# Reworking the first block's start: x0 by halves, a half-width V group, transposes inside groups, held x loads

## The chip, the cores and the metric

One core of one Trainium2 chip. The metric is the time of one execution in microseconds of device time, measured by repeated runs; the kernel before took 696.94 us (median of three runs, 696.61 to 697.02). The profile's span of an execution is 1.7 to 1.9 us shorter than its time in nearly all runs.

## The reference, cut to what matters

The program is a layer norm, a sliding-window attention with 32 heads, a residual, a second layer norm and a dense SiLU block, over x of 2048 rows by 1024 columns in bfloat16:

```python
qkv = layernorm(x) @ wqkv            # wqkv is 1024 x 3072: Q, K, V
o   = windowed_softmax(q k^T) v      # window 256
h   = x + o @ wo
out = h + silu(layernorm(h) @ w1) @ w2
```

Only the first 512 rows matter below: four tiles of 128 rows (tile 0 to 3) are loaded, normalized, transposed, and multiplied by the V columns of wqkv. Everything later waits for that.

## The kernel before

The loads at the start. All but one are issued by SyncE, in this order:

```python
nc.scalar.activation(out=dummy[:], in_=eps[:], func=ACT.Sqrt)   # loads the table early
load_x(0, 0)                       # 256 KB
load_wqkv(2 * D)                   # V columns 0-511, 1 MB
load_x(0, 1, nc.scalar)
load_x(0, 2)
load_wqkv(2 * D + 512)             # V columns 512-1023, 1 MB
load_x(0, 3)
load_wqkv(0)                       # first Q columns, 1 MB
...
for i in range(11):                # warm-up matmuls on zeros
    nc.tensor.matmul(o_ps[i % 2]..., lhsT=warm[:, 0, 0:P], rhs=warm[:, 0, :], start=True, stop=True)
```

The small tiles and the big buffers come from pools:

```python
small = ctx.enter_context(tc.tile_pool(name="small", bufs=2))
big = ctx.enter_context(tc.tile_pool(name="big", bufs=1))
...
r_w = big.tile([P, 28672], BF16, name="r_w")     # weights; then r_t, r_o (x), r_a, r_e, r_n
```

The first block. `ln_first` does statistics in two halves on VectorE, the square root on ScalarE, and a normalization in four pieces, so that TensorE can transpose piece by piece; `turn_first` makes eight transposes and four copies on ScalarE; `v_group` is eight matmuls of 512 columns and a copy:

```python
ln_first(x_ring[0], st, rs, 0, None, (x_ring[1], half))   # x1's first half fills the wait for the root
turn_first(x_ring[0], lnT_b[0], 0)
ln_first(x_ring[1], st, rs, 1, half)
v_group(0, 0, 0, act, turn_1)          # turn_1: tile 1's eight transposes before the last matmul
ln_first(x_ring[2], st, rs, 2)
v_group(0, 1, 0, act)
ln_first(x_ring[3], st, rs, 3)
ln_transpose(x_ring[3], lnT_b[0], 3)   # a DMA transpose, issued by SyncE
for c0 in (D, 512, D + 512):
    load_wqkv(c0)
v_group(0, 0, 1, act)
turn_first(x_ring[2], lnT_b[0], 2)
v_group(0, 1, 1, act)
v_group(0, 2, 0, act); v_group(0, 2, 1, act)
... v_group(0, 3, 0, act); v_group(0, 3, 1, act)
for j in range(4):
    load_x(1, j)                       # next block's x, slots 4 to 7
```

The softmax here doesn't subtract the row's maximum and nothing guards it: scores larger than these inputs give would overflow.

## Time and profile before

| what | us |
|---|---|
| time, median | 696.94 |
| span of the profiled run | 695.5 |
| x0 landed | 4.31 |
| first V matmul | 7.98 |
| end of the V phase | 23.26 |

Two rows of the issue table for the end of the first block are added here; the last column is the time from issue to landing.

```profile
r_w<-r_o SPq DMA_TRANSPOSE x1, 2.8
r_w<-in_A_wqkv_dram SPq DMA_DIRECT2D x1, 1024.0 KB, 8.8
```

The first is tile 3's DMA transpose (issued at 16.42), the second the first Q weights (issued at 5.50, so landed at 14.3). In every profile of this study but c3's, whose output was wrong, the span is the end of the V phase plus 672.1 to 672.3 us: what follows the V phase never differs. So a span tells, for any run, when its V phase ended.

### The profile page before, as it was taken

The page shows a single profiled execution, that of the slowest core. Times are in us where ns is not written, and L with a number is a line of the kernel's source. Part 1 is how long each engine was busy: PE and PEld are TensorE (multiplying, and loading weights), DVE is VectorE, ACT ScalarE, POOL GpSimd, SP SyncE. Part 2 cuts the span into 40 slices and gives each one's busy share as a digit, 9 for nine tenths or more (in the row PEclk, how much of TensorE's full clock was granted, in tenths as well). Part 3 has the DMA queues.
Part 4 walks back from the last instruction along what each step waited for, and adds up shares of the span by engine and source line. Part 5 has one row for each costly group of instructions (what it writes and reads, how often), then busy time and mean ns, then how long its engine had stood idle before and what let it go on. Part 6 is the DMA issues. An engine that isn't in the chain of part 4 may idle for free.

```text
span 695.5 us, 12334 instructions
## 1 busy us (share of the span) xinstructions
PE 690.1 (99%) x5091; PEld 331.6 (48%) x5091; DVE 289.5 (42%) x616; ACT 257.9 (37%) x328; POOL 174.5 (25%) x391
## 2 busy tenths in 40 slices
PE   8999999999999999999999999999999999999998
PEld 3444444555555555544444444444444444444445
DVE  6267646644443448544316134433133251244111
ACT  4326657777777777621310023300033100233000
POOL 1007667777777777500000000000000000000000
PEclk9999999999999999999999999999999999999999
DMA  7732131026231778880123410024200023100110
GB/s 241 257 53 77 35 93 51 17 60 193 70 124 23 205 251 272 199 311 31 31 76 99 107 38 1 1 83 77 83 1 1 11 95 91 45 1 1 30 39 24
DMA packets 76457, 60.84 MB, mean 87 GB/s; under 512 B 50288, under 2 KB 60528, under 8 KB 76400
## 3 DMA queue, kind: packets, MB, share of 16 engines
q1 hardware_dynamic: 76256, 59.78, 29.9%
q8 instruction: 40, 0.66, 0.4%
q10 hardware_dynamic: 144, 0.26, 0.1%
q14 instruction: 17, 0.14, 0.1%
HBM read 39.85 MB, written 8.39 MB: 69 GB/s over the span
## 4 chain that ended last, share of the span: by engine, by line
PE 99%; DMA 1%; DVE 0%; issue 0%
PE hacc L563 19%; PE hacc L600 17%; PE acc L248 16%; PE acc L600 10%; PE acc L563 9%; PE acc L238 8%; PE acc L267 7%; PE o_ps L339 4%; PE sc L285 3%; PE hacc L267 1%; PE o_ps L354 1%; PE sc L313 1%; DMA r_o<-in_A_x_dram 1%; PE tp L216 0%; DVE ln_st L169 0%; DVE r_o L197 0%
## 5 line engine op out<-in xcount | busy, mean ns | idle before, releaser
L330 POOL TENSOR_SCALAR_AFFINE_SELECT r_e<-r_e 128x256 bf16<-128x256 bf16 (+1 forms) x384 | 171.6, 477 | 116.5 <-ACT r_e L322 65.1
L293 ACT ACTIVATE r_e<-sc 128x1024 bf16<-128x1024 f32 x144 | 139.5, 1021 | 45.1 <-PE sc L285 31.0
L600 PEld LDWEIGHTS <-r_a 128*128 128x128 bf16 x952 | 90.9, 98 | 103.0
L563 PEld LDWEIGHTS <-r_w 128*128 128x128 bf16 x896 | 87.4, 98 | 104.8
L600 PE MATMUL hacc<-r_a 128*128 128x512 bf16 (+2 forms) x616 | 122.5, 360 | 0.0
L563 PE MATMUL hacc<-r_e,r_w 128*128 128x512 bf16 x456 | 100.9, 379 | 0.0
L572 ACT ACTIVATE r_n<-hacc 128x512 f32<-128x512 f32 x30 | 17.9, 597 | 178.9 <-PE hacc L563 178.9
L600 PE MATMUL acc<-r_a 128*128 128x512 bf16 x336 | 74.0, 379 | 0.0
L248 PEld LDWEIGHTS <-r_w 128*128 128x128 bf16 x512 | 46.5, 97 | 57.1 <-issue 7.0
L250 DVE CAST r_a<-acc 128x512 bf16<-128x512 f32 x56 | 38.7, 691 | 72.9 <-PE acc L248 56.3
L248 PE MATMUL acc<-r_t,r_w 128*128 128x512 bf16 x256 | 60.0, 379 | 0.0
L248 PE MATMUL acc<-r_w 128*128 128x512 bf16 x256 | 58.2, 380 | 0.0
L267 PE MATMUL acc<-r_o,r_a 128*128 128x512 bf16 x208 | 49.4, 380 | 0.0
L563 PE MATMUL acc<-r_e,r_w 128*128 128x512 bf16 x216 | 49.1, 379 | 0.0
L339 PEld LDWEIGHTS <-r_e 128*128 128x128 bf16 x1152 | 39.5, 96 | 17.0
L322 ACT ACTIVATE r_e<-sc 128x1024 bf16<-128x1024 f32 x36 | 34.9, 1021 | 21.2 <-PE sc L313 20.1
L339 PE MATMUL o_ps<-r_a,r_e 128*128 128x33 bf16 x1152 | 40.2, 178 | 0.0
L615 DVE SCALAR_TENSOR_TENSOR r_t<-hacc,r_t 128x512 bf16<-128x512 f32 (+2 forms) x22 | 14.0, 635 | 56.7 <-PE hacc L600 56.7
L267 PEld LDWEIGHTS <-r_a 128*128 128x128 bf16 x256 | 23.1, 98 | 29.6 <-issue 5.1
L615 DVE SCALAR_TENSOR_TENSOR r_t<-acc,r_t 128x512 bf16<-128x512 f32 x12 | 8.3, 692 | 64.2 <-PE acc L600 64.2
L573 DVE SCALAR_TENSOR_TENSOR r_a<-r_n,hacc 128x512 bf16<-128x512 f32 x30 | 20.6, 688 | 33.0 <-ACT r_n L572 33.0
L563 PE MATMUL hacc<-r_a,r_w 128*128 128x512 bf16 x144 | 32.9, 379 | 0.0
(71 smaller groups left out, 476.5 us busy)
## 6 DMA issues: line engine op xcount, KB each, us to landing
r_w<-in_B_w_dram SPq DMA_DIRECT2D x8, 896.0 KB, 5.1
r_a<-in_B_w_dram SPq DMA_DIRECT2D x7, 1024.0 KB, 7.9
r_w<-in_A_wqkv_dram SPq DMA_DIRECT2D x6, 1024.0 KB, 8.7
h_dram<-r_t SPq DMA_DIRECT2D x16, 256.0 KB, 3.0
r_t<-h_dram SPq DMA_DIRECT2D x16, 256.0 KB, 2.8
out_dram<-r_t SPq DMA_DIRECT2D x31, 128.0 KB, 1.7
r_o<-in_A_x_dram SPq DMA_DIRECT2D x15, 256.0 KB, 4.0
r_e<-h_dram SPq DMA_DIRECT2D x3, 1024.0 KB, 5.7
```

The lines of the kernel that those rows point to most:

```text
L238: nc.tensor.matmul(acc, lhsT=lnT_b[b % 2][:, kt, j * P:(j + 1) * P], rhs=wv[:, kt, c * 512:(c + 1) * 512], start=(kt == 0), stop=(kt == KT ...
L248: nc.tensor.matmul(acc, lhsT=wqk[:, kt, col0:col0 + P], rhs=lnT_b[b % 2][:, kt, :], start=(kt == 0), stop=(kt == KT - 1))
L250: copy(out=(qT, kT)[which][b][:, g, :], in_=acc)
L267: nc.tensor.matmul(acc, lhsT=qT[b][:, g, j * P:(j + 1) * P], rhs=wo[:, g, c * 512:(c + 1) * 512], start=(g == 0), stop=(g == G - 1))
L285: nc.tensor.matmul(sc[hh // 2][:, hh % 2, ch * P:(ch + nq) * P], lhsT=kT[t // 4][r0:r0 + DH, g, (t % 4) * P:(t % 4 + 1) * P], rhs=qT[b][r0 ...
L293: nc.scalar.activation(out=e, in_=sc[pair], func=ACT.Exp, scale=scale)
L322: nc.scalar.activation(out=e, in_=sc[pair], func=ACT.Exp, scale=scale)
L330: nc.gpsimd.affine_select(out=ap, in_=ap, pattern=[[0, 2], [0, n], [sgn, P]], compare_op=ALU.is_ge if upper else ALU.is_gt, fill=0.0, base ...
L339: nc.tensor.matmul(o_ps[pair][:, qt * 2 + hh, 0:VW], lhsT=e_of(i, kind, pair)[:, hh, ch * P:(ch + 1) * P], rhs=v[:, b * 4 + kt, g * 4 + pa ...
L563: nc.tensor.matmul(acc, lhsT=w1[:, kt, ft * P:(ft + 1) * P], rhs=ln2T[b][:, kt, :], start=(kt == 0), stop=(kt == KT - 1))
L600: nc.tensor.matmul(acc[:, 0:c1 - c0], lhsT=gT[:, ft, j * P:(j + 1) * P], rhs=w2[ft // 4][:, ft % 4, c0:c1], start=(ft == 0), stop=(ft == F ...
L615: nc.vector.scalar_tensor_tensor(out=t_out[j % 2][:, c0:c1], in0=acc[:, 0:c1 - c0], scalar=0.5, in1=t_in[j % 2][:, c0:c1], op0=ALU.mult, o ...
```

## The change

The intent: start TensorE earlier, by loading x0 in two halves on two queues; keep it busy while VectorE normalizes tile 1, by a V group of 256 columns right after the first; hide transposes inside groups; and keep the next block's x loads out of the way of tile 3's DMA transpose. The diff, cut to its core:

```diff
+    X_SLOT = (0, 0, 4, 0)                     # block 1's x now overwrites block 0's
-    load_x(0, 0)
-    load_wqkv(2 * D)
-    load_x(0, 1, nc.scalar)
-    load_x(0, 2)
-    load_wqkv(2 * D + 512)
+    for queue, c0 in ((nc.sync, 0), (nc.scalar, 512)):
+        queue.dma_start(out=x_ring[0][:, c0:c0 + 512], in_=x2d[0:P, c0:c0 + 512])
+    load_x(0, 1)
+    for queue, k0 in ((nc.scalar, 0), (nc.sync, 4)):
+        queue.dma_start(out=wv[:, k0:k0 + 4, 0:512], in_=wqkv_v[:, k0:k0 + 4, 2 * D:2 * D + 512])
+    for c0, k0, k1 in ((512, 0, 4), (512, 4, 8), (768, 0, 8)):
+        nc.sync.dma_start(out=wv[:, k0:k1, c0:c0 + 256], in_=wqkv_v[:, k0:k1, 2 * D + c0:2 * D + c0 + 256])
+        if c0 == 512 and k0 == 4:
+            load_x(0, 2)
...
-    for i in range(11):
+    for i in range(10):
...
+    quarters = small.tile([P, 4, 6], F32, name="ln_st1", tag="ln_st1")     # tile 1's statistics by quarters
...
+    v_group(0, 0, 0, act)
+    v_cols(0, 0, 512, 768, act, turn_at(1, (3, 5, 7)))
+    turn_first(x_ring[1], lnT_b[0], 1, 3)
+    ln_whole(x_ring[2], st, rs, 2, None, (x_ring[3], half))    # normalized in one piece
     v_group(0, 1, 0, act)
+    ln_whole(x_ring[3], st, rs, 3, half)
     ln_transpose(x_ring[3], lnT_b[0], 3)
+    v_cols(0, 0, 768, 1024, act)
+    v_group(0, 1, 1, act, turn_at(2, (2, 3, 4, 5)))
+    load_x(1, 3)                              # waits for tile 3's transpose; the rest stands behind it
+    load_wqkv(D)
+    for j in range(3):
+        load_x(1, j)
+    for c0 in (512, D + 512):
+        load_wqkv(c0)
```

More of the change, by code (lines that the diff above doesn't have):

```diff
@@ L137, in load_x @@
     def load_x(b, j, queue=nc.sync):
-        queue.dma_start(out=x_ring[(b % 2) * 4 + j], in_=x2d[(b * 4 + j) * P:(b * 4 + j + 1) * P, :])
+        queue.dma_start(out=x_ring[X_SLOT[b] + j], in_=x2d[(b * 4 + j) * P:(b * 4 + j + 1) * P, :])
     def load_wqkv(c0):
@@ L201, in ln_transpose, with ln_first, ln_quarter, ln_whole @@
         nc.sync.dma_start_transpose(out=dst[:, :, j * P:(j + 1) * P], in_=xt)
-    def ln_first(xt, st, rs, j, half_done=None, ahead=None):
+    def ln_first(xt, st, rs, j, stats, ahead=None):
+        nc.vector.bn_aggr(out=st[:, j, :], in_=stats[:])
+        nc.scalar.activation(out=rs[:, j:j + 1], in_=st[:, j, 1:2], func=ACT.Sqrt, bias=eps[:], scale=1.0)
+        if ahead is not None:
+            ahead()
+        nc.vector.reciprocal(out=rs[:, j:j + 1], in_=rs[:, j:j + 1])
+        for h in range(4):
+            ln_norm(xt[:, h * 256:(h + 1) * 256], st, rs, j)
+    def ln_quarter(xt, stats, c):
+        nc.vector.bn_stats(out=stats[:, c, :], in_=xt[:, c * 256:(c + 1) * 256])
+    def ln_whole(xt, st, rs, j, half_done=None, ahead=None):
         ln_stats(xt, st, j, half_done)
@@ L206, in ln_first, with turn_first @@
         if ahead is not None:
-            ln_half(ahead[0], ahead[1], 0)
+            ln_half(*ahead, 0)
         nc.vector.reciprocal(out=rs[:, j:j + 1], in_=rs[:, j:j + 1])
-        for h in range(4):
-            ln_norm(xt[:, h * 256:(h + 1) * 256], st, rs, j)
-    def turn_first(xt, dst, j):
-        for h in range(4):
-            for i in range(2):
-                kt = h * 2 + i
-                nc.tensor.transpose(out=tp_ps[h][:, i * P:(i + 1) * P], in_=xt[:, kt * P:(kt + 1) * P], identity=ident[:])
-            nc.scalar.copy(out=dst[:, h * 2:(h + 1) * 2, j * P:(j + 1) * P],
-                           in_=tp_ps[h][:, 0:256].rearrange("p (k q) -> p k q", q=P))
+        ln_norm(xt, st, rs, j)
+    def turn_first(xt, dst, j, h):
+        for i in range(2):
+            kt = h * 2 + i
+            nc.tensor.transpose(out=tp_ps[h][:, i * P:(i + 1) * P], in_=xt[:, kt * P:(kt + 1) * P], identity=ident[:])
+        nc.scalar.copy(out=dst[:, h * 2:(h + 1) * 2, j * P:(j + 1) * P],
+                       in_=tp_ps[h][:, 0:256].rearrange("p (k q) -> p k q", q=P))
     def ln_tiles(tag):
@@ L231, in next_acc, with v_cols @@
         return acc_banks[acc_n[0] % len(acc_banks)]
-    def v_group(b, j, c, copy, between=None):
-        acc = next_acc()
+    def v_cols(b, j, c0, c1, copy, between=None):
+        acc = next_acc()[:, 0:c1 - c0]
         for kt in range(KT):
@@ L237, in v_group @@
                 between(kt)
-            nc.tensor.matmul(acc, lhsT=lnT_b[b % 2][:, kt, j * P:(j + 1) * P], rhs=wv[:, kt, c * 512:(c + 1) * 512],
+            nc.tensor.matmul(acc, lhsT=lnT_b[b % 2][:, kt, j * P:(j + 1) * P], rhs=wv[:, kt, c0:c1],
                              start=(kt == 0), stop=(kt == KT - 1))
-        copy(out=v[:, b * 4 + j, c * 16:(c + 1) * 16, 0:DH], in_=acc.rearrange("p (h d) -> p h d", d=DH))
+        copy(out=v[:, b * 4 + j, c0 // DH:c1 // DH, 0:DH], in_=acc.rearrange("p (h d) -> p h d", d=DH))
+    def v_group(b, j, c, copy, between=None):
+        v_cols(b, j, c * 512, (c + 1) * 512, copy, between)
     def qk_group(b, which, g, copy, between=None):
@@ L387, with turn_at, between @@
     st, rs = ln_tiles("a")
-    half = small.tile([P, 2, 6], F32, name="ln_st", tag="ln_st")
-    ln_first(x_ring[0], st, rs, 0, None, (x_ring[1], half))
-    turn_first(x_ring[0], lnT_b[0], 0)
-    ln_first(x_ring[1], st, rs, 1, half)
-    def turn_1(kt):
-        if kt == 7:
-            turn_first(x_ring[1], lnT_b[0], 1)
-    v_group(0, 0, 0, act, turn_1)
-    ln_first(x_ring[2], st, rs, 2)
+    halves = small.tile([P, 2, 6], F32, name="ln_st", tag="ln_st")
+    quarters = small.tile([P, 4, 6], F32, name="ln_st1", tag="ln_st1")
+    for c in range(2):
+        ln_half(x_ring[0], halves, c)
+    ln_first(x_ring[0], st, rs, 0, halves, lambda: ln_quarter(x_ring[1], quarters, 0))
+    for h in range(4):
+        turn_first(x_ring[0], lnT_b[0], 0, h)
+    for c in range(1, 4):
+        ln_quarter(x_ring[1], quarters, c)
+    ln_first(x_ring[1], st, rs, 1, quarters)
+    def turn_at(j, when):
+        def between(kt):
+            if kt in when:
+                turn_first(x_ring[j], lnT_b[0], j, when.index(kt))
+        return between
+    v_group(0, 0, 0, act)
+    v_cols(0, 0, 512, 768, act, turn_at(1, (3, 5, 7)))
+    turn_first(x_ring[1], lnT_b[0], 1, 3)
+    half = small.tile([P, 2, 6], F32, name="ln_st", tag="ln_st")
+    ln_whole(x_ring[2], st, rs, 2, None, (x_ring[3], half))
     v_group(0, 1, 0, act)
-    ln_first(x_ring[3], st, rs, 3)
+    ln_whole(x_ring[3], st, rs, 3, half)
     ln_transpose(x_ring[3], lnT_b[0], 3)
-    for c0 in (D, 512, D + 512):
+    v_cols(0, 0, 768, 1024, act)
[5 more added lines that the diff above has]
+    for c0 in (512, D + 512):
         load_wqkv(c0)
-    v_group(0, 0, 1, act)
-    turn_first(x_ring[2], lnT_b[0], 2)
-    v_group(0, 1, 1, act)
     v_group(0, 2, 0, act)
@@ L416 @@
     sc = [sc_pool.tile([P, 2, 512], F32, name=f"sc{i}") for i in range(2)]
-    for j in range(4):
-        load_x(1, j)
     def ln1_steps(b):
         st, rs = ln_tiles("a")
-        xs = [x_ring[(b % 2) * 4 + j] for j in range(4)]
+        xs = [x_ring[X_SLOT[b] + j] for j in range(4)]
         steps = [lambda j=j: ln_stats(xs[j], st, j) for j in range(4)]
```

## The prediction

> **What bounds the kernel now**
>
> I read the page first, for whether the end is set by one engine, then the chain of waits over the first 45 us, then the timeline and the stretches of the same time.
>
> ```profile
> PE 690.1 (99%) x5091; PEld 331.6 (48%) x5091; DVE 289.5 (42%) x616; ACT 257.9 (37%) x328; POOL 174.5 (25%) x391
> PE   8999999999999999999999999999999999999998
> ```
>
> TensorE is busy 99% of 695.5 us; only the first and last slices fall short. Every instruction that the change touches belongs to the first block, so the question is how much earlier TensorE gets through its start. What follows it is a stream without gaps and should only shift.
>
> ```profile
> 0.81 3.51 DMA r_o<-in_A_x_dram
> 4.31 0.02 issue
> 4.33 1.30 DVE ln_st L169 x2
> 5.63 0.02 issue
> 5.66 0.21 DVE st_a L177
> 5.87 0.56 DVE ln_st L169
> 6.42 0.07 DVE rs_a L208
> 6.50 0.03 issue
> 6.52 0.36 DVE r_o L197
> 6.88 0.05 issue
> 6.93 1.06 PE tp L216 x8
> 7.98 1.51 PE acc L238 x7
> 9.49 1.01 PE tp L216 x8
> 10.51 3.67 PE acc L238 x17
> 14.18 0.45 PE tp L216 x8
> 14.62 8.63 PE acc L238 x40
> 23.26 21.80 PE acc L248 x101
> ```
>
> This is the chain: load of x tile 0 (3.51 us), statistics, square root, normalization, transposes, first V matmul at 7.98. Then TensorE alone carries it. From it come the unit costs: 40 matmuls in 8.63 us is 0.216 us each; eight transposes with operands ready take 0.45 (the row at 14.18). Those of tile 0 and tile 1 take 1.06 and 1.01, because they follow four quarter-width normalizations. So after 6.93 the start loses 0.61 + 0.56 us, and before it everything. The V phase ends at 23.26 = 7.98 + 64 x 0.216 + 1.01 + 0.45.
>
> ```profile
> 6.34 0.15 DVE L208 RECIPROCAL rs_a<-rs_a 128x1 f32<-128x1 f32 x1
> 6.52 1.12 DVE L197 TENSOR_SCALAR r_o<-r_o,st_a,rs_a 128x256 bf16<-128x256 bf16 x4
> ```
>
> The timeline gives the spacing on VectorE: the reciprocal starts at 6.34, the normalization runs 6.52 to 7.64 in four pieces 0.28 apart. In the second tile the aggregate ends at 8.49 and the reciprocal starts at 8.85: 0.36 is the bare detour over ScalarE. In the first tile it is 0.47, since the half of x1 put there (0.64) is longer than the gap.
>
> ```profile
> 2.00:3.00 1.00, 1.00 (x4) 0.41 (x3) 0.00 (x0) 0.28 (x2) 1.00 (x1) 1.00 0.97 248
> 4.00:5.00 1.00, 1.00 (x4) 0.36 (x3) 0.67 (x2) 0.00 (x0) 0.00 (x0) 1.00 1.08 385
> 12.00:13.00 1.00, 1.00 (x7) 0.46 (x5) 0.96 (x5) 0.51 (x1) 0.00 (x0) 1.00 1.08 385
> ```
>
> In the stretches the last two figures are DMA share and GB/s. The engines are full from 2 to 13.3 us, at 250 GB/s at first, then 385. The issue table by stretch gives landings (issue plus time to landing): x0 4.31, x1 4.87, V weights 0-511 7.56, V weights 512-1023 11.0, x3 11.6, first Q weights 14.3, tile 3's DMA transpose 16.42 + 2.8 = 19.2.
>
> **What the Trainium skill says**
>
> "DMA: Bandwidth & Descriptors", section "Issuing engines are not separate DMA queues": transfers from either sequencer run on the same 16 engines and interleave; a second issuer saves only issue time. The trace agrees in part: x1, issued by ScalarE at 0.97, lands 0.56 after x0, issued at 0.81. So two half loads on two queues are not twice as fast; what they save is issue time and other traffic ahead of them. The same page, "Specifications", gives 512 B as the least transfer for full rate. The 256-column weight pieces are runs of exactly that; the kernel before has no such runs from HBM, but its DMA transposes move smaller packets at 280 to 290 GB/s.
>
> "TensorE: Matmul & The Clock Gate", Part 1: warm start-to-start is N / 2.4 GHz + 2.5 ns, and an idle window of about 3.4 us is needed to fall back to half clock. The trace has 216 ns for 512 columns and 56 ns for 128. For 256 columns I estimate 109 ns from this page. One warm-up matmul less (0.43 us in the trace) leaves a gap of under 1 us, so I expect no cold start.
>
> "VectorE: DVE Perf Modes", the section on the TRN2 errata: a fixed latency per instruction, so short pieces pay more. Here: one 1024-wide normalization takes 0.54, four 256-wide ones 1.12; a 512-wide statistic 0.64, so I estimate 0.37 for 256 wide (about 0.1 fixed, taken from the smallest instructions of the trace).
>
> **The change part by part**
>
> 1. *x0 in halves, one per queue, x1 on SyncE third.* Removed: one 256 KB load and x1 beside it. Nothing but x0 is ahead now, but the same 256 KB go through the slow first stretch. I take 3.5 us for the first half and 3.9 to 4.1 for the second. The first half's statistic (0.65) lies beside the wait for the second; statistics end at about 4.8 where they ended at 5.63. Gain about 0.8.
> 2. *Gap filler.* A quarter of x1 (0.37) in place of a half (0.64), so the 0.47 could fall to 0.38. But VectorE works in order and x1 now lands at 5.0 to 5.3, by the bytes ahead of it, so the quarter may hold the reciprocal. I take the reciprocal at 5.6 (before: 6.34), a net gain of 0.73.
> 3. *Reciprocal to first V matmul*: unchanged, 7.98 - 6.34 = 1.64. First matmul at 7.25. The weights' two halves need to be there at 7.25 and 8.1: the same 1.57 MB are ahead of the second half as before, when they landed at 7.56; the first half, 0.5 MB less, should land at about 6.6. No stall.
> 4. *Half-width V group, transposes inside.* Before, TensorE had 7 matmuls (1.51) and then took 1.01 for tile 1's transposes. Now it has 8 matmuls (1.73) and 3 half-width ones (0.33) before the first pair: 9.31. VectorE: normalization of tile 0 5.78 to 6.90, three quarters 1.1, aggregate 0.25, square root detour 0.36, reciprocal 0.2: normalization of tile 1 from 8.8, first piece ready 9.2, then every 0.28; TensorE asks for the pieces every 0.33. All four fit, by about 0.1 us. The transposes cost 0.45: gain 0.56. Extra half-width matmuls: 8 x 2.5 ns, nothing.
> 5. *Weights 512-767 in two pieces, 768-1023 later.* Needed at 9.0, 9.6 and 12.0; by bytes ahead at 385 GB/s they land near 8.2, 8.9 and 11. Hidden, with little to spare.
> 6. *Tiles 2 and 3 normalized whole, transposes of 2 inside a group.* VectorE: tile 2 statistics from 9.9 to 11.4, half of x3 (landing 11.6) to 12.3, normalization to 13.0; TensorE asks at 7.25 + 1.73 + 0.86 + 0.45 + 1.73 + 0.86 + 0.43 = 13.31. Fits. Tile 3 is normalized by 15.0, its transpose issued then (before 16.42), landed at 17.8; needed two groups after tile 2, at 18.5. Fits with 0.7, before 0.6. The 0.58 per tile that whole normalization saves on VectorE keeps this margin, it isn't itself a gain.
> 7. *Next x loads behind tile 3's transpose, slots 0 to 3.* K weights now wait for the landing (17.8) and a 256 KB load: landed near 23.5, needed at 22 + 4 groups x 1.73 = 28.9. x of block 1 lands near 26, its statistics begin at about 30. Nothing on the path.
>
> Sum: 0.73 + 0.56 = 1.29; V phase ends at 7.25 + 64 x 0.216 + 2 x 0.45 = 21.97, where it was 23.26. I take off 0.1 for small stalls at parts 4 and 5: 1.2 us. 696.94 - 1.2 = 695.7.
>
> **The rivals**
>
> *A: more and smaller loads are slow at the start.* There are seven loads before x2 where there were three, and x loads run back to back later in the trace (four from 51.8 on) take about 1 us each at some 260 GB/s, a fixed cost each beside the bytes. If each extra load costs 0.3 us, x1 lands at 5.6 or later and the weights 512-1023 about 1 us later; the held reciprocal and a stall in the half-width group take back 0.5 to 1.2: time 696.2 to 697.0. For it: the slow first stretch. Against: the weights' 1 KB packets run at 385.
>
> *B: 512-byte packets at reduced rate.* At half rate, 1 MB takes 2.7 us more; the half-width group stalls about 0.6, x3 and the first Q weights land 1.3 to 2.7 late, tile 3's transpose goes out late behind them, and TensorE waits there for up to another 1 us: 696.5 to 697.5. Against: 256-byte packets at 280 GB/s.
>
> *C: the halves land much earlier.* With nothing beside it, x0 could land at 3.4, and x1 by 4.6: reciprocal at 5.1, gain 1.8: 695.1.
>
> *D: the gain is lost later,* as block 1 waits for x loads or K weights. Part 7 leaves 3 to 5 us, so I give it little.
>
> **Range and chances**
>
> The unsure terms are x0's landing (0.4 us either way), x1's (0 to 0.5 late), and the weights (0 to 1 late). The lower end takes rival C half-way: 694.7; the upper end takes A nearly whole: 696.7. A change of over 2% would be 14 us, as much as the whole start before steady work; nothing in either direction has that size: faster 0.01, same 0.98, slower 0.01.
>
> **What would show it right or wrong**
>
> In the chain of the changed kernel: first statistic before 4.0 and last by 4.9 (part 1); reciprocal about 5.6 without an idle wait for x1 before the quarter (2); first V matmul about 7.25 (3); no wait on normalization or weights between 7.25 and 13 and eight transposes at 0.45 (4, 5); the first group of tile 3 starting as soon as tile 2's end (6); Q groups from about 22.0 and everything after it at the old spacing, 1.3 earlier (7). Wrong, if x1 or the weights 512-767 are what TensorE or VectorE waits for (A, B), or if the gain at the end of the V phase is not found again at the end of the span (D).
>
> Predicted time 695.7 us, range 694.7 to 696.7.

## The result

| | before | the change |
|---|---|---|
| median, us | 696.73 (6 runs) | 698.63 (6 runs) |
| lowest and highest | 696.38, 697.02 | 696.63, 699.93 |
| spans of the six runs | | 694.8, 696.4, 696.8, 696.8, 697.8, 698.1 |

The ratio is 1.0028, with a 95% interval of 1.0012 to 1.0044. Ratios here are the mean time of one kernel's fast runs over that of the other's of the same rounds, so not quite the ratio of the medians. The change is slower by 1.9 us by the medians, and it spreads over 3.3 us where the kernel before spreads over 0.6. The predicted 695.7 and its range to 696.7 were missed.

The profile shown is of the slowest of the six, at 699.93. First the page: busy time by engine, and TensorE's busy tenths.

```profile
PE 686.6 (98%) x5011; PEld 333.2 (48%) x5098; DVE 288.9 (41%) x612; ACT 258.8 (37%) x329; POOL 175.2 (25%) x391
PE   7999999999999999999999999999999999999998
```

The loss is in the first slice alone (7 where it was 8). Next the chain of waits over the first 45 us:

```profile
1.24 8.10 DMA r_w<-in_A_wqkv_dram
9.34 0.04 issue
9.38 3.43 PE acc L254 x11
12.82 0.21 PE tp L232 x2
...
18.39 6.04 PE acc L254 x28
24.43 0.05 issue
24.48 1.46 PE acc L254 x6
25.94 9.28 PE acc L267 x43
```

The chain no longer begins with x0 but with a weight load: the first half of V columns 0-511, on ScalarE's queue, took 8.10 us and landed at 9.34, so the first V matmul is at 9.38 (it was 7.98; 7.25 was predicted). The V phase ends at 25.94 instead of 23.26: 2.68 later, and the span is 2.6 longer. One row of the waits says the same:

```profile
PE acc L254 <- DMA r_w<-in_A_wqkv_dram: 2.2, 1, 2.2
```

Then the rates. In the chain, 11 matmuls after 9.38 take 3.43 us. Eight of 512 and three of 256 columns take 2.05 at full clock. The stretches show why; their last three columns are the granted clock of TensorE, DMA share and GB/s:

```profile
8.00:9.00 1.00, 0.00 (x0) 0.00 (x0) 0.60 (x4) 0.30 (x1) 0.00 (x0) 1.00 1.21 313
11.00:12.00 1.00, 1.00 (x4) 0.32 (x3) 0.00 (x0) 0.00 (x0) 0.00 (x0) 0.50 1.10 333
12.00:13.00 1.00, 1.00 (x7) 0.78 (x6) 0.70 (x2) 0.59 (x1) 0.00 (x0) 0.50 1.09 358
```

TensorE stood still from 7.21 to 9.38, and from 10.21 to 13.62 the clock records grant half speed. And the DMA engines, as full as before, moved 313 to 358 GB/s where they had moved 385.

The early part of VectorE's work went as predicted: the timeline has the reciprocal of tile 0 at 5.58 (5.6 predicted, 6.34 before), then the normalization in four pieces.

```profile
5.58 0.15 DVE L214 RECIPROCAL rs_a<-rs_a 128x1 f32<-128x1 f32 x1
5.76 1.11 DVE L202 TENSOR_SCALAR r_o<-r_o,st_a,rs_a 128x256 bf16<-128x256 bf16 x4
```

A load runs on 16 DMA engines, and the trace records a completion of each. For the load that TensorE waited for they read, in us (from the trace's records, not one of the views):

```
5.78 5.85 5.86 5.89 5.98 5.99 6.05 6.06 6.12 6.20 6.26 6.29 6.34 6.34 6.35 9.34
```

Fifteen engines were done at 6.35; one came 3.0 us later, and in the loads after it 1.9 us after the others.

### The profile page after: what moved, and what is told of

Read it like the earlier page. It is cut to its first block, busy times and chain, and to the rows that moved or that the text cites. A ratio compares the mean times of both kernels' runs of the same rounds, so it can differ in the third digit from the quotient of the medians.

```text
span 698.1 us, 12261 instructions
## 1 busy us (share of the span) xinstructions
PE 686.6 (98%) x5011; PEld 333.2 (48%) x5098; DVE 288.9 (41%) x612; ACT 258.8 (37%) x329; POOL 175.2 (25%) x391
## 4 chain that ended last, share of the span: by engine, by line
PE 98%; DMA 1%; issue 1%; ACTq 0%; DVE 0%
PE hacc L630 21%; PE hacc L593 18%; PE acc L267 16%; PE acc L593 10%; PE acc L254 8%; PE acc L630 7%; PE acc L286 7%; PE o_ps L358 4%; PE sc L304 3%; PE hacc L286 1%; PE o_ps L373 1%; DMA r_w<-in_A_wqkv_dram 1%; PE sc L332 1%; PE tp L232 0%; ACTq L150 0%
## 5 line engine op out<-in xcount | busy, mean ns | idle before, releaser
L630 PE MATMUL hacc<-r_a 128*128 128x512 bf16 (+2 forms) x717 | 145.9, 362 | 0.6
L593 PE MATMUL hacc<-r_e,r_w 128*128 128x512 bf16 x432 | 95.7, 379 | 0.0
L602 ACT ACTIVATE r_n<-hacc 128x512 f32<-128x512 f32 x27 | 16.1, 598 | 175.5 <-PE hacc L593 175.5
L267 PE MATMUL acc<-r_t,r_w 128*128 128x512 bf16 x241 | 58.5, 379 | 0.8
L593 PE MATMUL acc<-r_e,r_w 128*128 128x512 bf16 x225 | 53.3, 379 | 0.7
L645 DVE SCALAR_TENSOR_TENSOR r_t<-hacc,r_t 128x512 bf16<-128x512 f32 (+2 forms) x26 | 16.7, 644 | 86.7 <-PE hacc L630 81.3
L630 PE MATMUL acc<-r_a 128*128 128x512 bf16 x220 | 48.8, 379 | 0.2
L254 PE MATMUL acc<-r_w 128*128 128x512 bf16 (+1 forms) x130 | 31.4, 381 | 2.5 <-DMA r_w<-in_A_wqkv_dram 2.2
L603 DVE SCALAR_TENSOR_TENSOR r_a<-r_n,hacc 128x512 bf16<-128x512 f32 x27 | 18.6, 688 | 29.9 <-ACT r_n L602 29.9
```

Source lines behind the costliest of these rows:

```text
L254: nc.tensor.matmul(acc, lhsT=lnT_b[b % 2][:, kt, j * P:(j + 1) * P], rhs=wv[:, kt, c0:c1], start=(kt == 0), stop=(kt == KT - 1))
L267: nc.tensor.matmul(acc, lhsT=wqk[:, kt, col0:col0 + P], rhs=lnT_b[b % 2][:, kt, :], start=(kt == 0), stop=(kt == KT - 1))
L593: nc.tensor.matmul(acc, lhsT=w1[:, kt, ft * P:(ft + 1) * P], rhs=ln2T[b][:, kt, :], start=(kt == 0), stop=(kt == KT - 1))
L603: nc.vector.scalar_tensor_tensor(out=gT[:, ft, :], in0=th, scalar=1.0, in1=acc, op0=ALU.add, op1=ALU.mult)
L630: nc.tensor.matmul(acc[:, 0:c1 - c0], lhsT=gT[:, ft, j * P:(j + 1) * P], rhs=w2[ft // 4][:, ft % 4, c0:c1], start=(ft == 0), stop=(ft == F ...
```

## The experiments

Each was run in 5 rounds against the kernel before on the same chip; the five batches ran on chips 13, 8, 15, 13 and 12. Where not said otherwise, outputs were correct.

### First batch: is it ScalarE's queue, the short rows, or the clock?

**b1.** Both halves of V columns 0-511 on SyncE.

```diff
-    for queue, k0 in ((nc.scalar, 0), (nc.sync, 4)):
+    for queue, k0 in ((nc.sync, 0), (nc.sync, 4)):
```

> The changed kernel, with both halves of V weights 0-511 issued by SyncE, in order, and none by ScalarE. Theory T: the load on ScalarE's queue landed at 9.34 because one of the 16 engines served that queue late beside SyncE's traffic (its sixteenth completion came at 8.79, the fifteenth at 5.93). In one queue the load stands ahead of the 256-column pieces on each engine, so the first half lands by 6.7, the second by 7.6; first V matmul at 7.2 to 7.5, no wait of TensorE on weights over 0.4 us, no half-clock window; time about 696.0 (695.6 to 696.6), and the spread of single runs falls from 3.3 us to under 1. Rival R1 (packets of 512 B are slow, and all loads are late with them): the halves land early as in T, but the wait moves to the half-width group, at 696.5 to 697.5. Rival R2 (simply too many bytes ahead): the first matmul stays after 8.5 us and the time above 698.

Measured: 700.05 (697.98 to 700.28; before 696.91), ratio 1.0036. Six engines lagged by up to 1.9 us and two by about 1, in every load from the weights on. Here the late x3 (14.40) and a DMA transpose of 4.8 us set the end of the V phase, 26.21. Theory T, ScalarE's queue, has fallen; what I had taken for a matter of one queue occurs on the other too.

**b2.** V columns 512-1023 in two loads with 1 KB rows in place of three with 512 B rows.

```diff
-    for c0, k0, k1 in ((512, 0, 4), (512, 4, 8), (768, 0, 8)):
-        ...
+    for k0 in (0, 4):
+        nc.sync.dma_start(out=wv[:, k0:k0 + 4, 512:1024], in_=wqkv_v[:, k0:k0 + 4, 2 * D + 512:2 * D + 1024])
+    load_x(0, 2)
```

> The changed kernel, with V weights 512-1023 loaded in two halves by rows of 512 columns (1 KB runs) in place of three loads of 256 columns (512 B runs); two queues as in the change. Theory T: the late engine on ScalarE's queue stays, first half of weights 0-511 lands after 8.5, first V matmul after 8.5 us, time 697.5 to 699.5, spread over 1.5 us. Rival R1 (small packets are the cause): the half lands by 7.5, time 695.5 to 696.5. In both, bulk transfer between 7 and 11 us goes up from some 310 to over 360 GB/s.

Measured: 698.73 (697.29 to 699.02), ratio 1.0021. One engine is late by 0.9 to 1.8 us; the first half of the weights lands at 8.32, then again a half-clock window, 7.70 to 11.11. So the late engine and the slow loads are there without the short rows. Even with 1 KB rows the first Q weights take 2.9 us on the engines that are on time, where they took 2.7 in the kernel before.

**b3.** Eleven more warm-up matmuls between tile 0's transposes and the first V matmul.

```diff
         turn_first(x_ring[0], lnT_b[0], 0, h)
+    for i in range(11):
+        nc.tensor.matmul(o_ps[i % 2]..., lhsT=warm[:, 0, 0:P], rhs=warm[:, 0, :], start=True, stop=True)
```

> The changed kernel, with 11 warm-up matmuls more, between the transposes of tile 0 and the first V matmul (2.4 us at full clock), so that TensorE isn't idle while it waits for the weights. If the half-clock window that follows the wait (records: 0.5 from 10.21 to 13.62) costs what its matmuls say (about 1.6 us: the matmuls there take 0.43 in place of 0.22), the slow runs at 699.8 go away, no window of 0.5 is left, and the time is 697.8 to 698.5 in all runs, with the first V matmul at 9.4 to 9.7 and the V phase over by 24.4 in place of 25.94. Rival: the clock isn't tied to the wait, the window of 0.5 and the times stay as in the change.

Measured: 698.23, all five runs within 698.19 to 698.29. No half-clock window; first V matmul at 9.48, V phase over at 24.21, which is 14.73 later, against 64 x 0.216 + 0.90 = 14.72. So with TensorE kept busy the clock stays up, which fits the size of the clock's part: the two runs of the change with a mean clock of 0.998 are at 699.77 and 699.93, three of the four others at 698.4 to 698.7. In this run no engine was late: the first weights were there at 6.37, and the filling itself held the start, so that the profiled run alone does not prove what the filling would do for a long wait. The x tiles were still late: x3 landed at 12.84, not 11.6.

**b4.** The kernel before with x0's halves alone.

```diff
-    load_x(0, 0)
+    for queue, c0 in ((nc.sync, 0), (nc.scalar, 512)):
+        queue.dma_start(out=x_ring[0][:, c0:c0 + 512], in_=x2d[0:P, c0:c0 + 512])
```

(with the dummy square root moved behind ScalarE's loads)

> The kernel before with x0 alone loaded in two halves, one on each queue (and the dummy square root behind ScalarE's two loads); everything else as before, with x1 on ScalarE's queue. Theory T: 0.26 MB of x1 on ScalarE's queue can lag on one engine as well, but it is needed only at 5.2 us for its first half, so the loss is small. x0's halves at 3.6 to 3.8, reciprocal at 5.6 to 5.8; V weights still at about 7.5, so the first V matmul is at 7.3 to 7.7 where it was at 7.98: time 696.0 to 696.7, gain 0.3 to 0.6. If x1 lands later than 5.2, the reciprocal waits for it and the gain is gone: 696.7 to 697.2.

Measured: 696.80 (696.67, 696.71, 696.80, 697.76, 698.65), ratio 1.0004. In the profiled run, of 696.67, the weights landed at 7.59, the first V matmul is at 7.63 and the V phase ends at 22.62, as expected. But the kernel before has a typical span of 695.0, that is a V phase over at 22.8: the profile that I predicted from, at 23.26, was one of its slower runs. Two of five runs were 1 to 2 us slower, and no profile shows why.

### Second batch: parts on the kernel before

**c1.** The kernel before with a changed front of loads: x0 in halves, x1 behind the second half, V columns 0-511 as two halves on SyncE.

```diff
-    load_x(0, 0)
-    load_wqkv(2 * D)
-    load_x(0, 1, nc.scalar)
+    for queue, c0 in ((nc.sync, 0), (nc.scalar, 512)):
+        queue.dma_start(out=x_ring[0][:, c0:c0 + 512], in_=x2d[0:P, c0:c0 + 512])
+    load_x(0, 1, nc.scalar)
+    for k0 in (0, 4):
+        nc.sync.dma_start(out=wv[:, k0:k0 + 4, 0:512], in_=wqkv_v[:, k0:k0 + 4, 2 * D:2 * D + 512])
```

> The kernel before with only the front of its loads changed: x0 in halves on the two queues, x1 behind the second half on ScalarE's queue, V weights 0-511 in two 1 KB-row halves on SyncE; everything else as before. The run with x0's halves alone had its first V matmul at 7.63, held by the weights that landed at 7.59, and a V phase over at 22.62. If that wait for all 1 MB is the next bound, the first half of the weights lands by 6.5, the first V matmul is at 7.2 to 7.35, the V phase ends at 22.2 to 22.4, and the time of runs without a late engine is 695.9 to 696.3 (kernel before 696.5 to 697.1 on the same chip). Rival: every further load costs some 0.2 us of all that follow, and a late engine is commoner with more loads: then the second half of the weights is the wait, the first matmuls stall after the fourth, and the median is 696.7 to 698.5.

Measured: 696.96 (696.65 to 697.60; before 696.74), ratio 1.0005. In the profile the first V matmul is at 7.23 and the V phase over at 22.50; no engine late. The step works and is worth less than I expected (695.9 to 696.3): tile 1's transposes again take 1.01.

**c2.** The kernel before with the 512 B rows, at the old place in the queue.

```diff
-    load_wqkv(2 * D + 512)
+    for c0, k0, k1 in ((512, 0, 4), (512, 4, 8), (768, 0, 8)):
+        nc.sync.dma_start(out=wv[:, k0:k1, c0:c0 + 256], in_=wqkv_v[:, k0:k1, 2 * D + c0:2 * D + c0 + 256])
```

> The kernel before with V weights 512-1023 in three loads by 256 columns (512 B runs) in place of one by 512, at the same place in the queue. Theory S (short rows move slower, whatever the order): the loads behind them land later by what 1 MB takes at 300 in place of 385 GB/s, 0.8 us: x3 at 12.3 to 12.6 (before 11.6), first Q weights at 15.0 to 15.3 (before 14.3), the weights 512-1023 complete at 11.6 to 12 (before 11.0). Rival: it is the order and number of the front loads that made all later; then the landings stay within 0.3 us of before. Needed at 14.4, so the time stays within 0.3 us of before in both, unless engines lag; if 512 B rows make an engine lag, one or more of the sixteen completions of a load come over 0.8 us after the others.

Measured: 697.05 (696.60 to 697.14), ratio 1.0004. The 1 MB landed at 11.09, x3 at 11.79, first Q weights at 14.49: each within 0.2 us of before. Theory S falls: three short-row loads take 2.98 us for the 1 MB, 0.28 more than the one load with 1 KB rows (2.70), and no engine lags. Yet in b3 the same loads had taken 3.5 us. Something else than their rows makes them slow in the change.

**c3.** The tail alone on the kernel before (next x loads held, tiles 2 and 3 normalized whole).

```diff
+    X_SLOT = (0, 0, 4, 0)
-    ln_first(x_ring[2], st, rs, 2)
+    ln_whole(x_ring[2], st, rs, 2, None, (x_ring[3], half))
     v_group(0, 1, 0, act)
-    ln_first(x_ring[3], st, rs, 3)
+    ln_whole(x_ring[3], st, rs, 3, half)
     ln_transpose(x_ring[3], lnT_b[0], 3)
+    load_x(1, 3)
+    load_wqkv(D)
+    ...
     v_group(0, 0, 1, act)
-    turn_first(x_ring[2], lnT_b[0], 2)
-    v_group(0, 1, 1, act)
+    v_group(0, 1, 1, act, turn_2)
```

> The kernel before with only the tail of the change: tiles 2 and 3 normalized whole, tile 2's transposes inside its V group, next x loads in slots 0 to 3 behind tile 3's DMA transpose. From the prediction: off the path, time within 0.3 us of before. The transpose is issued at about 15.2 (before 16.42). If it keeps its 2.8 us it lands at 18.0; but in the changed kernel it took 3.2, in the run with the filled gap 4.3 and with one queue 4.8 us. Rival: holding the loads back (or the queue behind the transpose being empty) makes the transpose itself slow, 4 us and more; it would land at 19.3 or later, beside a need at 19.8, and the time would still be within 0.5 us of before.

Measured: output wrong, 710.76. My error: the load of new x into slot 2 stood before tile 2's transposes in program order. Nothing follows from it; it was mended as e3.

**c4.** The change with the front of c1 (x1 on ScalarE's queue, both weight halves on SyncE's).

```diff
-    load_x(0, 1)
-    for queue, k0 in ((nc.scalar, 0), (nc.sync, 4)):
+    load_x(0, 1, nc.scalar)
+    for queue, k0 in ((nc.sync, 0), (nc.sync, 4)):
```

> The changed kernel with x1 on ScalarE's queue (behind the second half of x0) and both halves of V weights 0-511 on SyncE's: the front that the kernel before with a changed front has. If the front's order is what makes engines late, the first V matmul is at 7.2 to 7.5, and the time 696.0 to 697.2, held then by the loads of x2 and x3 behind the 512 B rows (x2 landing at 10.4, x3 at 12.9, where the prediction had 9.3 and 11.6): tile 2's transposes wait some 1 us for VectorE. If the short rows and the number of loads are it, this run is as late as the change: 697.5 to 700, with one or more completions over 0.8 us behind the others.

Measured: 698.38 (696.93, 698.14, 698.38, 698.59, 698.77), ratio 1.0021. The profiled run is the fast one: no engine late, first weights in time, and yet x3 at 12.61, for which VectorE waits, with the V phase over at 22.85. So the front isn't what matters, and the loads are slow even where no engine is late.

### Third batch: loads and order of work exchanged

**e1.** All loads of the change, order of work of the kernel before: the change's load block at the start, and then, against the change,

```diff
-    quarters = small.tile([P, 4, 6], F32, name="ln_st1", tag="ln_st1")
...
-    v_group(0, 0, 0, act)
-    v_cols(0, 0, 512, 768, act, turn_at(1, (3, 5, 7)))
+    v_group(0, 0, 0, act, turn_1)
...                                       # on as in the kernel before
```

> The loads of the change (all of its front: halves of x0, x1 on SyncE, V weights 0-511 on two queues, 512-1023 in 256-column pieces, x2 between them) with the order of work of the kernel before. In all runs so far the span is the end of the V phase + 672.2, so the span tells the end of the V phase. Theory L (the load program itself makes engines late): the first weights come at 8 to 9.5 in most runs, as in the change; spans of 696 to 697 in most runs (times 698 to 699). Theory E (the change's loads are late as often as those before; what differs is that its order of work asks for the 256-column pieces, x2 and x3 1.5 to 5 us sooner and so shows each lag): the order before needs only V weights 0-511 early, spans 694.6 to 695.4 in most runs, times 696.4 to 697.2.

Measured: 696.67 (696.37 to 697.03; before 696.79), ratio 0.9998. Its landings are close to the predicted ones: V columns 0-511 at 6.06 and 7.43, 512-767 at 8.18 and 8.93, x2 9.59, x3 11.74, first Q weights 14.44. The stretch from 12 to 13 us:

```profile
12.00:13.00 1.00, 1.00 (x6) 0.47 (x5) 0.96 (x5) 0.59 (x1) 0.00 (x0) 1.00 1.09 387
```

The load program of the change is not slow. Theory L falls.

**e2.** The order of work of the change, loads of the kernel before; against the change:

```diff
-    for queue, c0 in ((nc.sync, 0), (nc.scalar, 512)):
-        ...                               # the whole load block of the change
+    load_x(0, 0)
+    load_wqkv(2 * D)
+    load_x(0, 1, nc.scalar)
+    load_x(0, 2)
+    load_wqkv(2 * D + 512)
```

> The order of work of the change (half-width group second, transposes inside groups, tail held) with the loads of the kernel before. The columns 512-767 land with their whole 1 MB at 11.0, the half-width group asks for them at about 9.7: TensorE waits some 1.3 us; tile 1's transposes no longer wait 0.5. V phase over at 23.5 to 24, spans 695.7 to 696.2, times 697.4 to 698, and half-clock windows are few, as the wait is short. Theory E: late engines show as much as in the change, since this order has no slack either: spread over 1.5 us. Theory L: spread under 0.8 us.

Measured: 698.42 (698.29 to 698.50), ratio 1.0023. The half-width group waited 1.8 us for the columns that landed at 11.19, V phase over at 24.39. And the old loads are slow now:

```profile
12.00:13.00 1.00, 1.00 (x13) 0.73 (x11) 0.59 (x1) 1.00 (x4) 0.00 (x0) 1.00 1.09 348
```

348 GB/s against 387, on the same chip. So something that goes with the order of work slows the same loads, though no DMA instruction differs.

**e3.** The tail alone, mended: tile 2's transposes inside its group, the loads after it.

```diff
     ln_transpose(x_ring[3], lnT_b[0], 3)
-    for c0 in (D, 512, D + 512):
-        load_wqkv(c0)
     v_group(0, 0, 1, act)
-    turn_first(x_ring[2], lnT_b[0], 2)
-    v_group(0, 1, 1, act)
+    v_group(0, 1, 1, act, turn_2)
+    load_x(1, 3)
+    load_wqkv(D)
+    ...
```

> The tail alone again, mended: the run before it loaded new x into slot 2 before tile 2 had been transposed, in program order, and so computed something else. Now the loads come after that group. Expected as before: time within 0.3 us of the kernel before. The transpose is issued about 15.2; it lands at 18.0 if it keeps 2.8 us, at 19.2 or later if holding the loads back makes it slow (3.2 to 4.8 us in the runs with the held loads, 2.8 in those without).

Measured: 697.11 (696.95 to 697.12), ratio 1.0004. Transpose issued at 14.73, landed 2.8 us later; loads at the old rate (384 GB/s in that stretch). The tail is off the path, as predicted.

**e4.** c1 with ten warm-up matmuls and tile 1's transposes spread over two groups.

```diff
-    v_group(0, 0, 0, act, turn_1)
+    v_group(0, 0, 0, hold, turn_1((7,), 0))
+    turn_piece(x_ring[1], lnT_b[0], 1, 1)
+    v_group(0, 1, 0, hold, turn_1((1, 2), 2))
```

> A version meant to beat both: the kernel before with the front of the run that changed its front (first V matmul at 7.23 there), ten warm-up matmuls, and tile 1's transposes spread: the first pair before the last matmul of the first group, the second after it, the other two inside the second group of tile 0's columns, the copies of the V groups moved behind. In the front run these transposes took 1.01 in place of 0.45. Expected: first V matmul at 7.1 to 7.3, tile 1 costing 0.6 to 0.8 in place of 1.01, V phase over at 22.1 to 22.4, spans 694.3 to 694.7, times 696.1 to 696.6: 0.3 to 0.6 us below the kernel before. Rival: the pieces wait for ScalarE's copies, and nothing is gained on the front run: 696.7 to 697.2.

Measured: 696.62 (696.50, 696.53, 696.62, 696.95, 698.83), ratio 0.9997: no gain beyond the spread. Its profiled run is the slowest of the five, and shows one way in which such runs come about: TensorE got full clock only at 10.88, so that seven matmuls took 2.87 us. Where a profile has clock records (b3, e1 and f3 have none), they lie on a grid of 3.41 us whose phase differs from run to run. Here the warm-up fell across two such windows, busy for 73% and 68% of them, and neither was enough.

### What the slow loads have in common

Laying the completion times of 19 profiles side by side, one number splits them: the time from x3's landing to that of the first Q weights, 1 MB later on the queue. (c3 is left out; the profiles of the last two batches, told below, are included.) It is 2.69 to 2.71 us in ten kernels (before, b4, c1, c2, e1, e3, e4, and later f1, f3, g1) and 2.83 to 2.96 us in the other nine. Of the runs made so far, the slow ones are those with the change's tile for quarter statistics. That tile has two buffers of 96 B and stands ahead of the big buffers in memory. In the compiled program's memory map the weights' buffer starts at byte 17408 of each partition before, a multiple of 512, and at 17600 in the change: every big buffer is shifted by 192 B. "DMA: Bandwidth & Descriptors" in the Trainium skill, section "How a descriptor splits into AXI transactions", says that transfers are cut into transactions of 256 B at 256-byte boundaries, and that one which starts off such a boundary is fetched from the boundary below, which costs more (its example of 576 B needs four transactions in place of three). It says so of reads, and gives no rate; the last batches measure it.

### Fourth batch: the shift by itself

**f0.** The change again, unaltered, for the same rounds.

> The change itself, unaltered, for comparison on the same chip as the three others: 697.5 to 700 in most runs; 1 MB of first Q weights moved in 2.9 us or more, or one to several engines late by about 1 us or more.

Measured: 698.46 (696.59, 698.40, 698.46, 698.50, 698.83; before 696.80), ratio 1.0017.

**f1.** The change with the new tile padded to 256 B a buffer; the big buffers start at 17920, a multiple of 512.

```diff
-    quarters = small.tile([P, 4, 6], F32, name="ln_st1", tag="ln_st1")
+    quarters = small.tile([P, 64], F32, name="ln_st1", tag="ln_st1")[:, 0:24].rearrange("p (c s) -> p c s", s=6)
```

> The change with its new statistics tile padded from 96 to 256 B a buffer, of which the same 96 are used: the big buffers then start at multiples of 512 B, as before the change, and nothing else differs. Theory A (the shift of the buffers by 192 B slows and delays the loads): landings as in the run with the change's loads and the order of before (weights 0-511 at 6.1 and 7.4, columns 512-767 at 8.2 and 8.9, x2 9.6, x3 11.7, first Q weights 14.4), no engine over 0.6 us late, first V matmul at 7.2 to 7.5, V phase over at 22.0 to 22.5, times 696.0 to 696.7 with a spread under 1 us. Rival E (the order of work has no slack, the lag is there anyway): 697.5 to 700 as the change.

Measured: 697.07 (695.79, 695.93, 697.07, 697.38, 697.52), ratio to before 0.9999. The landings are those of theory A within 0.1 us (first weights 6.09 and 7.45, x3 11.72, first Q weights 14.43); the spread of 1.7 us, and the median with it, is a miss.

**f2.** The kernel before, shifted by 192 B by an unused tile.

```diff
+    pad = small.tile([P, 4, 6], F32, name="pad", tag="pad")
```

> The kernel before with one unused tile of two 96 B buffers, which shifts its big buffers by the same 192 B; no instruction differs. Theory A: 1 MB takes 2.9 us in place of 2.7 and engines lag in some runs; V weights 0-511 land at 7.8 or later and the median rises by 0.3 to 1.5 us, with single runs up to 699. Rival E: as before, within 0.2 us.

Measured: 696.79 (696.67 to 697.02), ratio 1.0001. The 1 MB took 2.96 us, as theory A says, but the median did not rise and no engine lagged in the loads of the first 12 us: here theory A's time was a miss.

**f3.** The change padded to 128 B a buffer; the big buffers start at 17664, a multiple of 256 but not of 512.

```diff
+    quarters = small.tile([P, 32], F32, name="ln_st1", tag="ln_st1")[:, 0:24].rearrange("p (c s) -> p c s", s=6)
```

> The change with the tile padded to 128 B a buffer: the big buffers start at multiples of 256 B but not of 512. If whole units of 256 B are what counts, it is as fast as the one padded to 256 (696.0 to 696.7). If it is 512 B, it is as slow as the change.

Measured: 695.99 (695.88, 695.96, 695.99, 697.08, 697.40), ratio 0.9995.

The stretch from 12 to 13 us, in f0, f1, f2 and f3, in this order:

```profile
12.00:13.00 1.00, 1.00 (x10) 0.80 (x9) 0.12 (x1) 0.85 (x2) 0.00 (x0) 1.00 1.07 356
```

```profile
12.00:13.00 1.00, 1.00 (x9) 0.60 (x7) 0.96 (x3) 0.48 (x1) 0.00 (x0) 1.00 1.08 386
```

```profile
12.00:13.00 1.00, 1.00 (x7) 0.41 (x5) 1.00 (x4) 0.47 (x1) 0.00 (x0) 1.00 1.09 347
```

```profile
12.00:13.00 1.00, 1.00 (x10) 0.67 (x7) 0.96 (x4) 0.56 (x1) 0.00 (x0) 1.00 1.09 387
```

356 and 347 GB/s with the shift, 386 and 387 without, in both orders of work. A multiple of 256 B is enough, 512 is not needed; whether 128 would do was not tried (17600 is a multiple of 64 only). In f2 not one instruction differs from the kernel before: the shift alone costs the loads about 10%, and lengthens tile 3's DMA transpose as well, from 2.81 to 3.18 us. There it costs no time, because that order of work has slack; in the change it does: f0 and f1 ran in the same rounds and differ by 1.4 us in their medians, and so do g2 and g1 below, which differ by the padding alone too. With 512 B rows the loss is larger: columns 512-767 took 0.86 and 0.89 us a piece in f0, 0.73 and 0.74 in f1. How x3, the last x tile, arrives in f0 and then in f1 (VectorE's timeline; in brackets its idle time before the instruction):

```profile
12.88 0.69 DVE L174 BATCH_NORM_STATS2 ln_st<-r_o 128x6 f32<-128x512 bf16 x1 [0.93 <-DMA r_o<-in_A_x_dram]
```

```profile
11.75 0.69 DVE L174 BATCH_NORM_STATS2 ln_st<-r_o 128x6 f32<-128x512 bf16 x1 [0.57 <-DMA r_o<-in_A_x_dram]
```

With the shift undone, x3 lands at 11.72, where the prediction had 11.6. The fast runs of f1 and f3 (spans 693.9 to 694.1, so V phases over at about 21.8) are what was predicted: 695.8 to 696.0 us. Half the runs are not. No profile is of a fast run; the end of f1's chain (rows of 0.05 us left out), in a run of 697.38, tells of a second item, and that of f3 (697.08) agrees:

```profile
15.07 4.65 DMA r_w<-r_o
19.77 3.63 PE acc L254 x16
23.39 11.65 PE acc L267 x54
```

Tile 3's DMA transpose went out at 15.07 (15.0 predicted) and took 4.65 us in place of 2.8; TensorE stood idle for 1.26 us before 19.77. By the completion records fifteen engines were done at 17.94 and the last at 19.72. In f0, with the shift, the same chain reads

```profile
16.19 4.97 DMA r_w<-r_o
21.21 3.63 PE acc L254 x16
24.84 10.36 PE acc L267 x48
```

### Fifth batch: does holding the loads make the transpose late?

**g1.** f1 with the tail undone alone.

```diff
-    X_SLOT = (0, 0, 4, 0)
...
     ln_transpose(x_ring[3], lnT_b[0], 3)
+    for c0 in (D, 512, D + 512):
+        load_wqkv(c0)
...
-    load_x(1, 3)
-    load_wqkv(D)
-    ...
```

> The change padded to 256 B, with its tail undone alone: the weight loads for Q and K stand right behind tile 3's DMA transpose in the queue, and block 1's x goes to slots 4 to 7 after the V phase, as in the kernel before. Theory H (holding the loads is what leaves the transpose's last engine late): the transpose lands 2.7 to 3.0 us after its issue, no wait of TensorE for it over 0.2 us, all runs at 695.7 to 696.4, spread under 0.7 us. Rival: the late completion has nothing to do with the loads behind it; two to three of five runs again at 697 to 697.5.

Measured: 697.04 (696.01, 696.92, 697.04, 697.32, 697.45; before 696.75), ratio 1.0004. The transpose, issued at 14.82, again took 4.6 us:

```profile
r_w<-r_o SPq DMA_TRANSPOSE x1, 4.6
```

with fifteen engines done at 17.69 and one at 19.38. Theory H has fallen: holding the loads isn't the cause.

**g2.** The change (with its shift), tail undone in the same way.

> The change itself (buffers shifted by 192 B), with its tail undone alone in the same way. Theory H with theory A: the slow loads stay (1 MB in 2.9 us and more, x3 landing at 12.6 to 12.9), the transpose lands about 3.0 us after its issue; runs at 696.6 to 697.3, apart from those in which an engine lags in the first 10 us. Rival: holding does not matter, most runs at 698.2 to 699 as the change.

Measured: 698.44 (697.22, 697.55, 698.44, 698.64, 698.78), ratio 1.0021: as the change. In the profiled run, of 697.55, the weights' last engine was 0.9 us late, x3 landed at 12.99, the transpose went out at 16.33 and took 3.5.

## Why the prediction was wrong

In a usual run of the change (most are at 698.4 to 698.8; the one profiled as f0 took 698.83) the failed step is part 6, tile 3's DMA transpose: it was issued 1.2 us late, because the loads of part 5 were slower than "385 GB/s", and took 5.0 us in place of 2.8. In the slowest runs part 3's "no stall" failed as well.

**Right: parts 1 to 4.** The halves of x0 landed at 3.61 and 3.77, statistics were over at 4.92, the reciprocal was at 5.58. Where the loads come in time (f1), the first V matmul is near 7.0 (7.25 predicted), and tile 1's transposes cost TensorE nothing but their own time. Tile 2's transposes began in f1 at 13.14 (13.31). The V phase that part by part came out at 21.97 is met by the fast runs of f1 and f3, at about 21.8. The tail (part 7) is free (e3). Not counted was that the profile I read was of a slow run, in which x0 landed at 4.31 (3.71 to 4.10 in c2, e2, e3 and f2, with the same load): measured from a typical V phase of the kernel before, 22.8, the step to 21.97 was worth 0.8, not 1.29.

**Wrong: the landings "by bytes ahead at 385 GB/s" (parts 5 and 6).** The rate isn't the change's: its own new tile shifts every big buffer by 192 B, and then 1 MB takes 2.9 us in place of 2.7, and 512 B rows 18 to 20% longer. In f0 x3 landed at 12.85, where I had 11.6, and tile 3's transpose went out at 16.19 instead of 15.0. I read the new tile as statistics and never asked where it lies. Rivals A and B had the right symptom, slow loads, and the wrong causes: c2 and e1 show that neither the rows (0.28 us for 1 MB) nor the number of loads does it.

**Wrong: "landed at 17.8 ... fits with 0.7" (part 6).** The transpose's 2.8 us holds in every profile without the shift and without a late engine (2.80 to 2.89); with the shift it is 3.1 to 3.5 up to the fifteenth engine (b3, 4.3, apart). In f0 it took 4.98: fifteen engines were done after 3.48, and the last came 1.49 later. Its group began at 21.21, not 18.5: 1.19 later issue, and 2.18 longer transfer, less the 0.7 of margin, make 2.67 of these 2.71. In f1 the issue was on time, and the longer transfer alone made 1.42 us at the end of the V phase (23.39 against 21.97). A sixteenth engine 1.5 to 1.8 us behind is found in 5 of 19 profiles (b1, f0, f1, f3, g1), with the shift and without, held and not held. No run isolates why, but the traces show what it goes with. Each page has a queue of kind "instruction" beside those of the program's own loads (queue, packets, MB, share of 16 engines):

```profile
q8 instruction: 40, 0.66, 0.4%
```

Each of its 40 packets is 16 KB and takes about 1 us; there is one for some 255 of TensorE's matmuls and weight loads. In all five profiles one such packet ran while tile 3's transpose was in flight (from 17.73 to 18.69 in f1), and the last completion came 1.03 to 1.11 us after the packet's end. Over the 19 profiles, 56 DMA transposes have a last engine more than 1.45 us behind the fifteenth; in 55 of them the last completion comes 1.0 to 1.25 us after the end of such a packet, in the 1,103 other transposes in 6. In the eight profiles in which that packet starts after tile 3's transpose has landed (at 20.5 to 25.3: before, b4, c1, c2, e1, e3, e4, f2) none is late; the change's order of work brings it to 17.1 to 20.8. It is not enough by itself: in after, b2, c4, e2 and g2 it started while the transpose was in flight too, and none was late; in b3 all sixteen engines came late together (4.3 us). No run moved this packet alone, so that it is the cause is not shown.

The kernel before has its need at 19.8 and mostly doesn't notice; the change moved that need to 18.5.

**Wrong in some runs: "No stall" (part 3) and "no cold start".** In the profiled run of the change one engine brought the first weights 3.0 us late; 9.38 against 7.25 is 2.13 of the loss. After the wait of 2.17 us the clock went to half, and the rest of the V phase lasted 16.56 where 14.72 was due: 1.84, of which the half-clock window alone, 3.41 us at half speed, is about 1.7. In the loads that land before 16 us, an engine 0.9 us or more behind the one before it, or a group of engines (b1), appears in 4 of the 9 shifted profiles (the change, b1, b2, g2) and in none of the 10 others. That is weak evidence for the shift as the cause, and no run isolates it. Late engines as such do not need the shift: in the loads issued from 17.8 us on, one engine is 0.8 to 1.4 us behind in seven profiles without it (before, b4, c1, c2, e1, e3, e4), there beside the 16 KB packet told of above. In the first 16 us no such packet runs, so what holds an engine there stays open.

**The size of it.** For a usual run of the change: from 697.07 to 698.46 (the medians of f1 and f0; 697.04 and 698.44 for g1 and g2) is the shift. From the 695.9 of f1's and f3's fast runs to 697.07 is, if their other slow runs are like the two profiled ones, the transpose's late engine, in about half of the runs. Padded, the change isn't shown to beat the kernel before: f3's median is 0.8 us lower (695.99 and 696.80), but the interval of its ratio, 0.9983 to 1.0008, holds 1, and f1 and g1 have no lower median than before. None of the 18 runs beats both kernels beyond doubt.

## What to carry to other kernels

A new small tile ahead of large buffers moves them: look at the memory map as well as at the instructions, and keep buffers that are filled by DMA at multiples of 256 B. A margin of 0.7 us on one transfer is not a margin when single engines come 1.5 us late in every fourth profile; look also at the DMA traffic that is not the program's own, which moves when the order of work does. Judge a schedule by the spread of its runs and not by one profile. A loss that stays with the order of work when the loads are exchanged, though no load differs, is not yet a property of the order: look for what else came along with it.

## What the Trainium skill lacked or had wrong

- "DMA: Bandwidth & Descriptors", section "How a descriptor splits into AXI transactions", gives the 256 B rule for reads and without a rate. Here destinations 192 B off a multiple of 256 brought HBM loads with rows of 1 KB and more from 385 to 387 GB/s down to 347 to 356, and 512 B rows from 0.74 to about 0.88 us per 256 KB; a start at 256 but not at 512 was as fast as one at 512 (387).
- "SBUF — State Buffer", section "Operand start alignment", treats alignment as a matter of what is legal, and says itself that speed was not timed. The pools' order and a 96 B tile are enough for the loss above.
- "TensorE: Matmul & The Clock Gate", Part 1, speaks of an idle window before the clock falls. Windows of 3.41 us in which TensorE was busy for 37% (the change) and 58% (b2) were followed by half clock, windows of 62% (e2), 64% (b1) and 71% (before) were not, but neither were later ones of 54% (f0, from 19.08) and 59% (b1, from 19.18), so that a window's busy share does not decide it alone; from half clock, 68% and 73% did not release it (e4), 80% did (b2). The free-running phase that the section describes agrees.
- No page that I looked at gives a figure for the spread of a transfer's sixteen completions: mostly 0.1 to 0.8 us, with a single engine 0.9 to 3.0 us late in some runs, which is what the waiting engine sees.
- Nor what an instruction queue's packets may cost the program's own transfers: here 40 of 16 KB, 0.9 to 2.1 us each, and beside them 55 of the 56 transposes with a last engine over 1.45 us behind.
